# Giving out the side work of the last two-path block in finer pieces, and reordering a second product

## The chip, the cores and the metric

The kernel runs on one core of one Trainium2 chip. The metric is the device time of one execution in microseconds (us), from a launch that does everything on the chip: the inputs lie in device memory, and the output is written back to it. TensorE (PE) does the matrix products, VectorE (DVE), ScalarE (ACT) and GpSimd (POOL) the elementwise work, and SyncE (SP) issues most transfers. The engines run side by side, each through its own list of instructions in order, and wait for one another by semaphores.

## The reference, cut to what matters

```python
def reference(...):                       # B = 2, S = 768, D = 512, 8 heads of 64
    x = attention(q, k, v)                # local window of 96 and 8 global keys
    # layer 1
    u = x + (U V applied along the sequence, rank 32)
    x = u + relu(u @ w_ch1) @ w_ch2       # w_ch1 512 x 2048, w_ch2 2048 x 512
    # layer 2
    u = x + real(fft(fft(x, axis=1), axis=2))
    un = (u - mean) / sqrt(var + 1e-6)
    return u + relu(un @ w_ch1') @ w_ch2'
```

The tokens of both batches are 1536 rows, cut into 12 tiles of 128: tiles 0 to 5 are batch 0, tiles 6 to 11 batch 1.

## The kernel before

**Precision.** A product of two float32 operands is made from three products of rounded parts: high by high, high by low, low by high. So every operand is split: a rounded copy (the "hi" tile, on ACT) and the rest (the "lo" tile, on DVE or POOL by a subtraction). Names: `wh`, `wo` are the parts of a weight tile, `gh`, `gl` of the relu's output, `uT..` of the transposed tokens.

**Blocks and chunks.** `ffn` walks over chunks c = 0 to 63 of 16 chunks a block; a block is four token tiles (512 tokens). Chunks 0 to 47 are layer 1, blocks 0 to 2, and chunks 48 to 63 are layer 2, block 0 (tiles 0 to 3, all of batch 0). A chunk has 12 matmuls at L201, which fill one accumulator `ps_h`, then ACT makes `gh` (L208) and DVE `gl` (L209) from it; and 12 matmuls at L224, which add the chunk before to the four accumulators `ps_acc`. So chunk c's L201 runs ahead of chunk c-1's L224. `w_split` makes a chunk's weights ready: ACT `wh` (L171), then POOL `wo` (L174, two pieces). `ffn` is a generator that stops four times a chunk.

**The other eight tiles of layer 2** (4 to 11) are not run as blocks but as the "unit" at the end (`unit`): 512 tokens stand for tiles 4 to 7 and 512 for tiles 8 to 11, and a scheme of the Strassen kind makes the first product of both from seven products of half matrices. Those need, from each pair of tiles (4+i, 8+i), the sums T1 to T4 of halves of the transposed tokens, split in hi and lo in the tiles `op0`, `op1`. The unit takes eight rounds p of two weight chunks. A round has 42 matmuls of the first product (L948), then four relus, q = 0 to 3, and 48 matmuls of the second product (L994): for each of eight tiles t and each of two weight chunks f three matmuls, which read relu number `f * 2 + t // 4`. The four `ps_acc` buffers hold the sums, and DVE adds each to `xall` (L1000), or in the last round makes the output (L252, L256) and sends it.

**Work beside a block.** `drive` runs `ffn` for 64 steps, a block, and lets a second generator, the side work, advance by `per` pieces per step on the average. During layer 2, block 0 the side work is the transform of batch 1 (`fft(1)`: 23 pieces, after a few empty ones of `lead`, which waits until layer 1 is done), and then `unit_tokens`, which normalizes, transposes and splits tiles 4 to 11. The names of the transform: `fold` makes on DVE, from sums and differences of the rows (L743, L746, L725, L726, L730), the operands `ee` and `oo` (hi by ACT L733, lo by DVE L738); PE multiplies them with tables (L775, L779, L786, L799, later L812, L825). `norm_one` takes mean and variance on DVE (L849, L850), the root on POOL (L851, L852), and writes the normalized tile `vb` on DVE (L854) into one of two halves of the buffer `vb0`; PE transposes it (L273 in `transpose_in`, L888 for the second tile of a pair); ACT copies the halves to `qk` (L882, L889, L890); POOL makes T1 to T4 (L892 to L895); ACT and DVE split them (L899, L900).

**Order.** The order in which the program is written is not quite the order of the engines: a scheduler goes over it and places each instruction in its engine's list, taking ready work ahead of work whose inputs it expects later. Instructions marked `keep` stay in the order written. All matmuls of `unit` are so marked; those of `ffn` and of the side work are not.

Of the kernel before, what the change touches and what calls it, by code (L numbers as in the profile page):

```python
# [10 lines left out]
ALU = mybir.AluOpType  # L11
AF = mybir.ActivationFunctionType

P = 128
B, H, S, HD = 2, 8, 768, 64
D = H * HD
# [4 lines left out]
NF = FF // P  # L21
# [17 lines left out]
class Prog:  # L39
# [801 lines left out]
        nc.vector.tensor_tensor(X[0:1, 511:256:-1], pc[0:1, 1:256], xm[0:1, 511:256:-1], ALU.add)  # L841
        yield

    def norm_one(self, i):
        nc, cp = self.nc, self.cp
        X = self.x[i]
        bs = cp.tile([P, 6], F32, tag="bs", bufs=2, name=f"bs{i}")
        mv = cp.tile([P, 2], F32, tag="mv", bufs=2, name=f"mv{i}")
        nc.vector.bn_stats(bs, X)  # L849
        nc.vector.bn_aggr(mv, bs)  # L850
        nc.gpsimd.tensor_scalar(mv[:, 1:2], mv[:, 1:2], 1.0e-6, None, ALU.add)  # L851
        nc.gpsimd.tensor_tensor(mv[:, 1:2], mv[:, 1:2], self.mh, ALU.pow)  # L852
        un = self.vb[0][:, (i % 2) * D:(i % 2 + 1) * D]
        nc.vector.tensor_scalar(un, X, mv[:, 0:1], mv[:, 1:2], ALU.subtract, ALU.mult)  # L854
        return un

    def norm(self, tiles):
        for i in tiles:
            un = self.norm_one(i)
            yield  # L860
            self.transpose_in(1, i, un)
            yield
# [5 lines left out]
    def unit_open(self, ctx):  # L868
        self.op = ctx.enter_context(self.tc.tile_pool(name="op", bufs=1))
        self.opu = [self.op.tile([P, 10, 512], FR, name=f"op{z}") for z in range(2)]  # L870

    def unit_tokens(self):
        nc = self.nc
        for i in range(4):
            st = self.qkb[i % 2]
            q0, q1 = st[:, 0:256], st[:, 256:512]
            T1, T2, T3, T4, b22 = (st[:, 512 + z * 256:768 + z * 256] for z in range(5))
            b12 = st[:, 1792:2048]
            un = self.norm_one(4 + i)
            yield  # L880
            tp = self.transpose_in(1, 4 + i, un)
            nc.scalar.copy(st[:, 0:512], tp)  # L882
            yield
            un = self.norm_one(8 + i)
            yield
            tp = self.psum("tr")
            for dd in range(ND):
                nc.tensor.transpose(tp[:, dd * P:(dd + 1) * P], un[:, dd * P:(dd + 1) * P], self.ident)  # L888
            nc.scalar.copy(b12, tp[:, 0:256])  # L889
            nc.scalar.copy(b22, tp[:, 256:512])  # L890
            yield
            nc.gpsimd.tensor_tensor(T1, b12, q0, ALU.subtract)  # L892
            nc.gpsimd.tensor_tensor(T3, b22, b12, ALU.subtract)
            nc.gpsimd.tensor_tensor(T2, T3, q0, ALU.add)
            nc.gpsimd.tensor_tensor(T4, q1, T2, ALU.subtract)  # L895
            yield
            hi, lo = (t[:, :, i * P:(i + 1) * P] for t in self.opu)
            src = st[:, 512:1792].rearrange("p (n q) -> p n q", n=10)
            nc.scalar.copy(hi, src)  # L899
            nc.vector.tensor_tensor(lo, src, hi.bitcast(F32), ALU.subtract)  # L900
            yield

    def unit_load(self, p):
# [28 lines left out]
    def unit(self):  # L932
        nc, keep = self.nc, self.tc.keep_in_program_order
# [7 lines left out]
        for p in range(NF // 2):  # L941
# [20 lines left out]
            X, Z, Y = self.psum("h"), self.psum("h"), self.psum("m")  # L962
# [20 lines left out]
            self.unit_load(p + 2)  # L983
            wh, wo = self.uw[p, 2]
            acc = {}
            order = [(0, 1), (1, 1), (0, 0), (1, 0)] + [(t, f) for t in range(2, 8) for f in (0, 1)]
            for t, f in order:
                first = t not in acc
                if first:
# [13 lines left out]
def drive(main, n, side, per):  # L1003
    acc = 0.0
    for _ in range(n):
        next(main)
        acc += per
        while acc >= 1.0 and side is not None:
            acc -= 1.0
            if next(side, "end") == "end":  # L1010
                side = None
    if side is not None:
        drain(side)


def lead(pg, n):
    while pg.n_done < n:
        yield


def chain(*gens):
    for g in gens:
        if callable(g):
            g = g()
        if g is not None:
            yield from g


def arm(tc, pg, fast):
# [59 lines left out]
    with ExitStack() as ctx4, ExitStack() as ctx3:  # L1089
        pg.fft_open(ctx3)  # L1090
        drive(main, 64, chain(pg.tr_gen(0, range(8, 12), pg.x), pg.fft_tables()), 0.3)
        drive(main, 64, chain(lead(pg, 6), pg.fft(0), pg.norm(range(0, 4))), 0.58)
        drive(main, 64, chain(lead(pg, 12), pg.fft(1), lambda: (ctx3.close(), pg.unit_open(ctx4), None)[2],
                              pg.unit_tokens()), 0.85)
        drain(main)


# [5 lines left out]
def drain(g):  # L1103
    for _ in g:
        pass


def program(tc, a):
    with ExitStack() as ctx:
        pg = Prog(tc, a)  # L1110
        pg.open(ctx)

        pg.setup(ctx)
        rv = tc.nc.values_load(pg.flag[0:1, 0:1], min_val=0, max_val=1)
        with tc.If(rv > 0) as cmp:
            arm(tc, pg, True)
        with cmp.Else():
            arm(tc, pg, False)
# [114 lines left out]
```

## Time and profile before

| | before |
|---|---|
| median of 3 runs | 685.51 us (681.99 to 686.04) |
| profiled execution, its time | 685.0 us |
| its span, first to last instruction | 683.1 us |
| mean granted TensorE clock | 0.992 |
| PE busy | 653.2 us (96%) |
| DVE busy | 420.3 us (62%) |
| ACT busy | 298.2 us (44%) |
| POOL busy | 334.6 us (49%) |

The profile is of one execution; 1.9 us of its time lie outside the span. An engine's busy time is the union of its instructions' spans; matmuls overlap one another, since one starts before the one ahead has left the array, so the pitch from start to start says what a matmul costs. In this execution, layer 2, block 0 takes from about 396 us to 511 us, and the unit from 511 us to the end.

### The profile page before, as it was taken

The numbers are of one execution on the slowest core, as the hardware profiler recorded it, in microseconds if no ns is written. First come the engines' busy times: TensorE is split into PE (matmuls) and PEld (weight loads), VectorE is DVE, ScalarE is ACT, GpSimd is POOL, SyncE is SP. The second block draws the span as 40 slices with busy tenths as digits, with TensorE's granted clock in tenths as the row PEclk, the third lists the DMA queues.
The fourth block names the chain that finished last, engine by engine and source line by source line (L and its number), as shares of the span: only waits on it lengthen the run. The fifth ranks groups of instructions, "written<-read, shape, count | busy, mean of one in ns | idle before, by whom it ended". The sixth has DMA issues, their size and how long they took to land.

```text
span 683.1 us, 9548 instructions
## 1 busy us (share of the span) xinstructions
PE 653.2 (96%) x3442; PEld 535.2 (78%) x3442; DVE 420.3 (62%) x770; ACT 298.2 (44%) x586; POOL 334.6 (49%) x336
## 2 busy tenths in 40 slices
PE   5998899999999999999999999999889999999996
PEld 4877686888778888888887777887668888888885
DVE  4789778998839534396388574474434544554544
ACT  4879874544435434344334323234433442224420
POOL 4002403546676555555356564357676644656410
PEclk8999999999999999999999999999999999999999
DMA  5588715778896877666463652111002111011003
GB/s 201 202 322 303 244 48 156 238 249 253 284 343 201 259 258 253 233 220 214 162 211 128 251 191 87 62 62 61 32 35 90 62 62 48 15 62 61 1 2 128
DMA packets 32841, 107.50 MB, mean 157 GB/s; under 512 B 3920, under 2 KB 6160, under 8 KB 29712
## 3 DMA queue, kind: packets, MB, share of 16 engines
q1 hardware_dynamic: 31248, 103.01, 44.2%
q0 software_dynamic: 1392, 3.65, 1.7%
q8 instruction: 29, 0.48, 0.3%
q14 instruction: 28, 0.23, 0.1%
q10 hardware_dynamic: 144, 0.13, 0.1%
HBM read 86.75 MB, written 20.02 MB: 156 GB/s over the span
## 4 chain that ended last, share of the span: by engine, by line
PE 53%; DVE 10%; POOL 6%; issue 3%; ACT 2%; DMA 2%; SPq 0%; DVEq 0%; POOLq 0%; ACTq 0%
PE ps_acc L994 13%; PE ps_acc L224 13%; PE ps_h L201 13%; PE ps_h L948 10%; POOL wo L174 2%; DVE wr L160 2%; DVE w L162 2%; PE ps_sd L948 2%; DVE gl L209 1%; DMA ur<-wscr 1%; ACT wr L156 1%; PE ps_sd L799 1%; PE ps_sd L775 1%; DMA w<-wscr 1%; POOL mv L852 1%
## 5 line engine op out<-in xcount | busy, mean ns | idle before, releaser
L174 POOL TENSOR_TENSOR wo<-w,wh 128x512 fp32r<-128x512 f32 x128 | 188.5, 1495 | 151.6 <-ACT wh L171 144.7
L201 PE MATMUL ps_h<-uT,wh 128*128 128x512 f32 x512 | 160.2, 393 | 0.4 <-DVE xall L592 0.4
L171 ACT CAST wh<-w 128x1024 fp32r<-128x1024 f32 x64 | 67.4, 1053 | 115.7 <-PE ps_acc L224 50.4
L201 PEld LDWEIGHTS ps_h<-uT,wh 128*128 128x128 f32 x512 | 94.5, 188 | 20.1 <-issue 1.6
L224 PE MATMUL ps_acc<-wh,gl 128*128 128x512 f32 x256 | 101.3, 396 | 2.4 <-DVE gl L209 2.1
L201 PE MATMUL ps_h<-uT,wo 128*128 128x512 f32 x256 | 100.4, 392 | 3.0 <-POOL wo L174 3.0
L224 PE MATMUL ps_acc<-wh,gh 128*128 128x512 f32 x256 | 102.0, 398 | 1.2 <-ACT gh L208 1.2
L224 PE MATMUL ps_acc<-wo,gh 128*128 128x512 f32 x256 | 100.3, 392 | 0.0
L209 DVE SCALAR_TENSOR_TENSOR gl<-ps_h,gh 128x512 fp32r<-128x512 f32 x64 | 43.8, 685 | 78.1 <-ACT gh L208 77.9
L929 POOL TENSOR_TENSOR uo<-ur,uh 128x256 fp32r<-128x256 f32 (+1 forms) x40 | 41.8, 1053 | 65.2 <-ACT uh L926 65.2
L208 ACT ACTIVATE gh<-ps_h 128x512 fp32r<-128x512 f32 x64 | 38.2, 597 | 61.4 <-PE ps_h L201 61.4
L224 PEld LDWEIGHTS ps_acc<-wh,gl 128*128 128x128 f32 x256 | 48.3, 189 | 15.3 <-DVE gl L209 5.0
L201 PEld LDWEIGHTS ps_h<-uT,wo 128*128 128x128 f32 x256 | 48.0, 188 | 15.0 <-POOL wo L174 4.7
L1000 DVE TENSOR_TENSOR xall<-ps_acc,xall 128x512 f32<-128x512 f32 x56 | 38.7, 692 | 32.9 <-PE ps_acc L994 32.8
L224 PEld LDWEIGHTS ps_acc<-wh,gh 128*128 128x128 f32 x256 | 48.5, 189 | 10.8 <-ACT gh L208 1.6
L224 PEld LDWEIGHTS ps_acc<-wo,gh 128*128 128x128 f32 x256 | 48.6, 190 | 9.7 <-issue 0.2
L160 DVE SCALAR_TENSOR_TENSOR wr<-wr 128x1024 int32<-128x1024 int32 x32 | 47.4, 1482 | 10.6 <-ACT wr L156 9.5
L537 ACT ACTIVATE p<-p,m 128x256 f32<-128x256 f32 (+2 forms) x96 | 47.6, 498 | 8.9 <-DVE m L525 8.9
L926 ACT CAST uh<-ur 128x256 fp32r<-128x256 f32 (+1 forms) x40 | 18.8, 488 | 74.9 <-PE ps_acc L994 68.9
L948 PE MATMUL ps_h<-op,uh 128*128 128x512 f32 x160 | 49.8, 392 | 0.0
L525 DVE CUSTOM_DVE_ANT_0 p<-ps_acc,dist 128x256 f32<-128x256 f32 (+2 forms) x96 | 34.9, 419 | 3.2 <-ACT pt L555 1.9
L156 ACT ACTIVATE wr<-wr 128x1024 f32<-128x1024 f32 x32 | 36.7, 1147 | 0.0
(263 smaller groups left out, 1142.4 us busy)
## 6 DMA issues: line engine op xcount, KB each, us to landing
w<-wscr SPq DMA_DIRECT2D x48, 512.0 KB, 4.3
wr<-wl SPq DMA_DIRECT2D x17, 1024.0 KB, 8.2
wr<-wl SPq DMA_DIRECT2D x60, 256.0 KB, 5.4
wscr<-w SPq DMA_DIRECT2D x16, 512.0 KB, 9.0
wscr<-wd SPq DMA_DIRECT2D x16, 512.0 KB, 3.0
ur<-wscr SPq DMA_DIRECT2D x16, 512.0 KB, 4.4
qk<-qkg SPq DMA_DIRECT2D x7, 1088.0 KB, 7.4
vb<-vw SPq DMA_DIRECT2D x8, 768.0 KB, 5.0
```

The lines of the kernel that those rows point to most:

```text
L156: keep(nc.scalar.activation(hi.bitcast(F32), hi.bitcast(F32), AF.Copy, scale=2.0 ** -112))
L160: nc.vector.scalar_tensor_tensor(lo, hi, 3, lo, ALU.logical_shift_left, ALU.bitwise_or)
L171: nc.scalar.copy(hi, raw)
L174: nc.gpsimd.tensor_tensor(lo[:, h], raw[:, h], hi[:, h].bitcast(F32), ALU.subtract)
L201: nc.tensor.matmul(hp, lhsT=w[:, s], rhs=u[:, dd, :], start=n == 0, stop=n == 11)
L209: nc.vector.scalar_tensor_tensor(gl, hp, 0.0, gh.bitcast(F32), ALU.max, ALU.subtract)
L224: nc.tensor.matmul(acc[t], lhsT=g[:, s], rhs=w[:, D:2 * D], start=pf == 0 and m == 0, stop=pf == NF - 1 and m == 2)
L537: keep(nc.scalar.activation(T[z][:, s], T[z][:, s], AF.Exp, bias=m[:, z, y:y + 1], scale=-1.0, accum_out=sm[:, u % 2, y, z:z + 1]))
L929: nc.gpsimd.tensor_tensor(lo[:, s], src, hi[:, s].bitcast(F32), ALU.subtract)
L948: keep(nc.tensor.matmul(out, lhsT=x[:, s], rhs=y[:, kt, :], start=start and kt + n == 0, stop=kt + n == 3, skip_group_check=not start))
L994: keep(nc.tensor.matmul(acc[t], lhsT=x[:, s], rhs=y[:, w], start=first and n == 0, stop=not first and n == 2))
L1000: nc.vector.tensor_tensor(self.x[4 + t], acc[t], self.x[4 + t], ALU.add)
```

## The change

Four things change.

1. The rate of the side work beside layer 2, block 0 goes from 0.85 to 1.25 pieces a step. The transform, whose 23 pieces are as they were, so takes 18 steps in place of 27.
2. `unit_tokens` was five steps for each of four pairs of tiles, a pair after the other. It is now 24 steps over all eight tiles, each followed by an empty piece (48 pieces), in an order in which tile k+1 is normalized (N) ahead of tile k's transposition (X), and the sums (T) and the split (H) of a pair come later still.
3. T1 to T4 are made on DVE in place of POOL. And `norm_one` takes the half of `vb0` from its caller: the two tiles of a pair had the same half, now they have one each.
4. In the unit's second product the three-matmul groups go in runs of four tiles: tiles 0 to 3 with the second chunk (f = 1), the same with the first, then tiles 4 to 7 likewise. In the last round tiles 4 to 7 are still finished one by one.

```diff
-    def norm_one(self, i):
+    def norm_one(self, i, z):
...
-        un = self.vb[0][:, (i % 2) * D:(i % 2 + 1) * D]
+        un = self.vb[0][:, z * D:(z + 1) * D]
...
     def unit_tokens(self):
         nc = self.nc
-        for i in range(4):
+        un = {}
+
+        def parts(i):
             st = self.qkb[i % 2]
-            un = self.norm_one(4 + i)
-            yield
-            tp = self.transpose_in(1, 4 + i, un)
-            nc.scalar.copy(st[:, 0:512], tp)
-            yield
-            un = self.norm_one(8 + i)
-            yield
...
-            nc.gpsimd.tensor_tensor(T1, b12, q0, ALU.subtract)
-            nc.gpsimd.tensor_tensor(T3, b22, b12, ALU.subtract)
-            nc.gpsimd.tensor_tensor(T2, T3, q0, ALU.add)
-            nc.gpsimd.tensor_tensor(T4, q1, T2, ALU.subtract)
-            yield
+        def N(k):
+            un[k] = self.norm_one(4 + k // 2 + k % 2 * 4, k % 2)
+
+        def X(k):
...
+        def T(i):
+            st, (q0, q1, T1, T2, T3, T4, b22, b12) = parts(i)
+            nc.vector.tensor_tensor(T1, b12, q0, ALU.subtract)
+            nc.vector.tensor_tensor(T3, b22, b12, ALU.subtract)
+            nc.vector.tensor_tensor(T2, T3, q0, ALU.add)
+            nc.vector.tensor_tensor(T4, q1, T2, ALU.subtract)
+
+        def H(i):
...
+        for n in "N0 N1 X0 N2 X1 T0 N3 X2 H0 N4 X3 T1 N5 X4 H1 N6 X5 T2 N7 X6 H2 X7 T3 H3".split():
+            {"N": N, "X": X, "T": T, "H": H}[n[0]](int(n[1]))
+            yield
             yield
...
-            order = [(0, 1), (1, 1), (0, 0), (1, 0)] + [(t, f) for t in range(2, 8) for f in (0, 1)]
+            order = [(t, f) for f in (1, 0) for t in range(4)]
+            if p < NF // 2 - 1:
+                order += [(t, f) for f in (1, 0) for t in range(4, 8)]
+            else:
+                order += [(t, f) for t in range(4, 8) for f in (1, 0)]
...
-                              pg.unit_tokens()), 0.85)
+                              pg.unit_tokens()), 1.25)
```

Neither the number of PE's instructions nor their shapes change. How the lists of the engines differ is shown at three places; the number behind a name is that of the chunk, of the tile or of the batch, and the one after the underscore a running number of the buffer.

PE, where the first product of the transform of batch 1 (L775) stands, before: behind all of chunk 50's L201 and chunk 49's L224.

```order
L224 MATMUL ps_acc_3886<-wh49_3802,gh49_3874 128x512
L224 MATMUL ps_acc_3886<-wo49_3803,gh49_3874 128x512
L224 MATMUL ps_acc_3886<-wh49_3802,gl49_3875 128x512
L775 MATMUL ps_sd_3973<-c10_2160,ee1_3859 128x386
L775 MATMUL ps_sd_3973<-c11_2161,ee1_3859 128x386
L775 MATMUL ps_sd_3973<-c10_2160,ee1_3859 128x386 x2
L775 MATMUL ps_sd_3973<-c11_2161,ee1_3859 128x386
L201 MATMUL ps_h_3986<-uT100_3565,wh51_3905 128x512
```

The same in the changed kernel:

```order
L201 MATMUL ps_h_3933<-uT100_3565,wo50_3855 128x512
L775 MATMUL ps_sd_3951<-c10_2160,ee1_3845 128x386
L775 MATMUL ps_sd_3951<-c11_2161,ee1_3845 128x386
L775 MATMUL ps_sd_3951<-c10_2160,ee1_3845 128x386 x2
L775 MATMUL ps_sd_3951<-c11_2161,ee1_3845 128x386
L201 MATMUL ps_h_3933<-uT100_3565,wh50_3854 128x512
```

It now stands in the middle of chunk 50's L201, 18 matmuls of 512 columns earlier; DVE's and ACT's lists ahead of it are nearly as they were.

DVE, the last pairs of the tokens' part, before:

```order
L900 TENSOR_TENSOR op1_4289<-qk0_64,op0_4288 128x10x128
L854 TENSOR_SCALAR vb0_68<-xall1_186,mv11_4635 128x512
L276 TENSOR_TENSOR uT111_4304<-ps_sd_4610,uT110_4303 128x4x128
L209 SCALAR_TENSOR_TENSOR gl61_4625<-ps_h_4603,gh61_4624 128x512
L900 TENSOR_TENSOR op1_4289<-qk1_65,op0_4288 128x10x128
L209 SCALAR_TENSOR_TENSOR gl62_4677<-ps_h_4659,gh62_4676 128x512
L209 SCALAR_TENSOR_TENSOR gl63_4720<-ps_h_4706,gh63_4719 128x512
```

The same in the changed kernel, where the last tile's `vb` stands six rows ahead of the first row shown:

```order
L209 SCALAR_TENSOR_TENSOR gl60_4579<-ps_h_4561,gh60_4578 128x512
L276 TENSOR_TENSOR uT111_4253<-ps_sd_4601,uT110_4252 128x4x128
L209 SCALAR_TENSOR_TENSOR gl61_4630<-ps_h_4616,gh61_4629 128x512
L898 TENSOR_TENSOR qk1_65<-qk1_65 128x256
L899 TENSOR_TENSOR qk1_65<-qk1_65 128x256
L900 TENSOR_TENSOR qk1_65<-qk1_65 128x256
L901 TENSOR_TENSOR qk1_65<-qk1_65 128x256
L908 TENSOR_TENSOR op1_4211<-qk1_65,op0_4210 128x10x128
L209 SCALAR_TENSOR_TENSOR gl62_4677<-ps_h_4659,gh62_4676 128x512
L209 SCALAR_TENSOR_TENSOR gl63_4720<-ps_h_4706,gh63_4719 128x512
```

The split (L900 before, L908 now) no longer stands right ahead of a `vb` (L854), and the four sums (L898 to L901) have come to DVE.

POOL, the same place, before:

```order
L174 TENSOR_TENSOR wo62_4597<-w62_4539,wh62_4596 128x512 x2
L174 TENSOR_TENSOR wo63_4655<-w63_4601,wh63_4654 128x512 x2
L892 TENSOR_TENSOR qk1_65<-qk1_65 128x256
L893 TENSOR_TENSOR qk1_65<-qk1_65 128x256
L894 TENSOR_TENSOR qk1_65<-qk1_65 128x256
L895 TENSOR_TENSOR qk1_65<-qk1_65 128x256
L929 TENSOR_TENSOR uo00_4699<-ur0_4541,uh00_4698 128x256
```

And in the changed kernel:

```order
L174 TENSOR_TENSOR wo60_4499<-w60_4450,wh60_4498 128x512 x2
L174 TENSOR_TENSOR wo61_4549<-w61_4503,wh61_4548 128x512 x2
L174 TENSOR_TENSOR wo62_4610<-w62_4553,wh62_4609 128x512 x2
L174 TENSOR_TENSOR wo63_4655<-w63_4614,wh63_4654 128x512 x2
L941 TENSOR_TENSOR uo00_4699<-ur0_4555,uh00_4698 128x256
```

POOL's sums for the last pair, which stood behind the low part of chunk 63's weights, are gone from its list.

## Rows read from the trace of the kernel before

**Rows 1.** PE's waits, 395 to 512 us: us in total, times, longest.

```profile
PE ps_sd L888 <- DVE vb L854: 2.2, 2, 1.2
PE ps_sd L775 <- ACT ee L733: 1.7, 1, 1.7
PE ps_acc L224 <- ACT gh L208: 1.2, 1, 1.2
PE ps_h L201 <- POOL wo L174: 1.0, 1, 1.0
PE ps_acc L224 <- DVE gl L209: 0.9, 1, 0.9
```

**Rows 2.** Stretches: us, busy of PE, PEld, DVE, ACT, POOL, PEclk, DMA share, GB/s.

```profile
398.00:413.00 15.00, 14.04 (x64) 11.46 (x62) 14.94 (x26) 4.98 (x9) 8.85 (x10) 1.00 0.54 193
450.00:500.00 50.00, 46.82 (x220) 37.69 (x219) 26.30 (x39) 20.04 (x32) 35.45 (x43) 1.00 0.14 52
500.00:512.00 12.00, 9.88 (x36) 7.36 (x35) 5.52 (x7) 5.19 (x11) 7.80 (x10) 0.86 0.11 40
512.00:600.00 88.00, 88.00 (x383) 71.38 (x382) 41.95 (x60) 31.66 (x65) 49.29 (x52) 1.00 0.16 60
```

**Rows 3.** Timeline of PE at the transform's start: start us, us, what.

```profile
404.00 0.61 PE L201 MATMUL ps_h<-uT,wh 128*128 128x512 f32 x2
...
409.44 1.04 PE L775 MATMUL ps_sd<-c,ee 128*128 128x386 f32 x5
...
413.75 0.91 PE L775 MATMUL ps_sd<-c,ee 128*128 128x386 f32 x3 [1.71 <-ACT ee L733]
```

**Rows 4.** Timeline of DVE, the same stretch.

```profile
405.73 1.51 DVE L725 TENSOR_TENSOR qk<-qk 128x255 f32<-128x255 f32 x1
407.16 1.25 DVE L726 COPY qk<-qk 128x2 f32<-128x2 f32 x1
...
412.15 0.68 DVE L209 SCALAR_TENSOR_TENSOR gl<-ps_h,gh 128x512 fp32r<-128x512 f32 x1
412.75 0.41 DVE L725 TENSOR_TENSOR qk<-qk 128x255 f32<-128x255 f32 x1
```

**Rows 5.** Timelines of POOL and of ACT, the same stretch.

```profile
405.38 3.00 POOL L174 TENSOR_TENSOR wo<-w,wh 128x512 fp32r<-128x512 f32 x2 [0.21 <-ACT wh L171]
...
408.44 0.41 ACT L733 CAST ee<-qk 128x258 fp32r<-128x258 f32 x1 [3.14 <-DVE qk L726]
```

**Rows 6.** Timeline of PE, the tokens' part: its waits, and a slow stretch behind them.

```profile
468.82 0.66 PE L888 MATMUL ps_sd<-ident,vb 128*128 128x128 f32 x4 [0.97 <-DVE vb L854]
...
479.66 0.50 PE L201 MATMUL ps_h<-uT,wo 128*128 128x512 f32 x1 [0.96 <-POOL wo L174]
...
492.57 0.66 PE L888 MATMUL ps_sd<-ident,vb 128*128 128x128 f32 x4 [1.25 <-DVE vb L854]
...
502.65 0.50 PE L224 MATMUL ps_acc<-wh,gh 128*128 128x512 f32 x1 [1.22 <-ACT gh L208]
...
504.28 0.50 PE L224 MATMUL ps_acc<-wh,gl 128*128 128x512 f32 x1 [0.90 <-DVE gl L209]
...
505.53 0.63 PE L224 MATMUL ps_acc<-wh,gh 128*128 128x512 f32 x1
505.96 0.63 PE L224 MATMUL ps_acc<-wo,gh 128*128 128x512 f32 x1
```

**Rows 7.** Timelines of ACT and DVE, the last pair of the tokens' part.

```profile
500.84 1.26 ACT L899 CAST op<-qk 128x1280 fp32r<-128x1280 f32 x1 [5.12 <-POOL qk L895]
502.01 0.59 ACT L208 ACTIVATE gh<-ps_h 128x512 fp32r<-128x512 f32 x1
...
502.13 1.49 DVE L900 TENSOR_TENSOR op<-qk,op 128x1280 fp32r<-128x1280 f32 x1 [7.17 <-ACT op L899]
```

**Rows 8.** POOL's sums by line: duration ns min/median/max, first and last start.

```profile
L895 POOL TENSOR_TENSOR qk<-qk x4: 731/736/742, 463.1 to 500.1; 128x256 f32<-128x256 f32 x4
```

**Rows 9.** The page, part 5: us busy, mean ns, idle before.

```profile
L1000 DVE TENSOR_TENSOR xall<-ps_acc,xall 128x512 f32<-128x512 f32 x56 | 38.7, 692 | 32.9 <-PE ps_acc L994 32.8
```

More of the change, by code (lines that the diff above doesn't have):

```diff
@@ L858, in norm @@
         for i in tiles:
-            un = self.norm_one(i)
+            un = self.norm_one(i, i % 2)
             yield
@@ L873, in unit_tokens @@
         nc = self.nc
-        for i in range(4):
+        un = {}
+        def parts(i):
             st = self.qkb[i % 2]
-            q0, q1 = st[:, 0:256], st[:, 256:512]
-            T1, T2, T3, T4, b22 = (st[:, 512 + z * 256:768 + z * 256] for z in range(5))
-            b12 = st[:, 1792:2048]
-            un = self.norm_one(4 + i)
-            yield
-            tp = self.transpose_in(1, 4 + i, un)
-            nc.scalar.copy(st[:, 0:512], tp)
-            yield
-            un = self.norm_one(8 + i)
-            yield
-            tp = self.psum("tr")
+            return st, [st[:, z * 256:z * 256 + 256] for z in range(8)]
+        def N(k):
+            un[k] = self.norm_one(4 + k // 2 + k % 2 * 4, k % 2)
+        def X(k):
+            st, (q0, q1, T1, T2, T3, T4, b22, b12) = parts(k // 2)
+            if k % 2 == 0:
+                tp = self.transpose_in(1, 4 + k // 2, un.pop(k))
+                nc.scalar.copy(st[:, 0:512], tp)
+                return
+            u, tp = un.pop(k), self.psum("tr")
             for dd in range(ND):
-                nc.tensor.transpose(tp[:, dd * P:(dd + 1) * P], un[:, dd * P:(dd + 1) * P], self.ident)
+                nc.tensor.transpose(tp[:, dd * P:(dd + 1) * P], u[:, dd * P:(dd + 1) * P], self.ident)
             nc.scalar.copy(b12, tp[:, 0:256])
             nc.scalar.copy(b22, tp[:, 256:512])
-            yield
-            nc.gpsimd.tensor_tensor(T1, b12, q0, ALU.subtract)
-            nc.gpsimd.tensor_tensor(T3, b22, b12, ALU.subtract)
-            nc.gpsimd.tensor_tensor(T2, T3, q0, ALU.add)
-            nc.gpsimd.tensor_tensor(T4, q1, T2, ALU.subtract)
-            yield
+        def T(i):
[5 more added lines that the diff above has]
+        def H(i):
+            st, _ = parts(i)
             hi, lo = (t[:, :, i * P:(i + 1) * P] for t in self.opu)
```

## Prediction

> **What bounds the kernel now.** I looked first at the busy time by stretch, then at PE's waits in the block that the change touches, then at the timelines around each wait. In the unit PE is busy for all of the 88 us from 512 to 600 us at the full granted clock [rows 2], so no wait there has anything to give. In layer 2, block 0 it is not: PE loses 3.2 of 50 us in the tokens' part and 2.1 of 12 us at its end, where the granted clock is 0.86 as well [rows 2]. PE's number of matmuls is the same in both kernels, so the change is worth what it does to waits, and to the clock behind them. The view of waits lists all that PE waits for between 395 and 512 us: 2.2 us for normalized tiles (`vb`), 1.7 for the transform's operand `ee`, 1.2 for `gh`, 1.0 for `wo`, 0.9 for `gl`, together 7.0 [rows 1].
>
> **What the change removes: the tokens' part.** Both waits for `vb` (0.97 and 1.25 us [rows 6]) come about since `vb` (L854) stands in DVE's list behind the split (L900), which waits for ACT's cast (L899), and that for POOL's sums: at the last pair ACT waits 5.12 us for POOL, and DVE 7.17 us for ACT [rows 7]. In the new order a tile's `vb` comes a whole step earlier, and its half of the buffer is not the one that the tile ahead still holds. Following the new lists by hand, with 0.227 us for a matmul of 512 columns (24 of them between 404.00 and 409.44 us [rows 3]), every `vb` but the first is done more than 5 us ahead of its transposition. So 2.2 us go. The wait for `wo` (0.96 us [rows 6]) came of POOL's list: four sums of 0.74 us [rows 8], 2.9 us, stood between the weight splits. They are gone from it, so 1.0 us goes.
>
> At the end of the block the chain is T on POOL, cast on ACT until 502.10, `gh` on ACT behind it (502.01), `gl` on DVE behind the split that starts at 502.13 [rows 7]; PE waits 1.22 us for the one and 0.90 for the other. Then the clock falls: two neighbouring matmuls start 0.43 us apart (505.53 and 505.96 [rows 6]) where the usual pitch is 0.227. The stretch's clock of 0.86 over 12 us [rows 2] is 3.4 us at 1.2 in place of 2.4 GHz, 1.7 us of work. In the new kernel T stands on DVE right behind ACT's copies, where nothing else queues. In the trace ACT had made the copies of the last pair 3.15 us after its transposition (492.57 [rows 6]) began, at 500.84 - 5.12 = 495.72 [rows 7]. The four sums take 4 x 0.41 = 1.6 us, by the fold's sum of nearly the same shape on DVE [rows 4], or up to 6 us if each meets a POOL instruction as the same line does at 405.73 (1.51 us [rows 4]). I take the short ones, since POOL's own sums are gone and its weight splits so end sooner. Cast 1.26 and `gh` 0.59 follow [rows 7]: `gh` of chunk 62 is there 6.6 us after the transposition, and PE wants it after four transposes (0.4 us) and 36 matmuls (8.2 us), 2.0 us later. `gl` needs split 1.49 [rows 7] and 0.68 [rows 4] after the cast, 8.2 us, and is wanted 0.45 us after `gh`, 0.8 us later. So both waits go, the second with little to spare, and with them the reason for the clock to fall: 1.2 + 0.9 + 1.7 = 3.8 us. I leave 0.4 us for new waits over the whole part (bounds 0 and 2: none by the lists, or both waits at the end as they were). Removed in all: 2.2 + 1.0 + 3.8 = 7.0 us, less 0.4.
>
> **What it costs: the transform's start.** At 1.25 pieces a step the first L775 stands 18 matmuls, 4.1 us, earlier in PE's list: behind six L201 that start at 404.00, so at 405.36 in place of 409.44 [rows 3]. Its operands come no earlier, since DVE is busy for 14.94 of the 15 us from 398 to 413 us [rows 2] and its list is the same up to there. The fourth matmul wants the second third of `ee`, which ACT has at 408.44 + 0.41 = 408.85 [rows 5]. PE is there at 405.36 + 3 x 0.18 = 405.9 (five of them took 1.04 us [rows 3]): a wait of 3.0 us where there was none. Then come two L775, six L201 (1.4 us), one more L775 at about 410.7 (0.2 us of wait for its low part), four L224 (0.9 us), and the L775 on the last third of `ee`. That was ready at 413.75 [rows 3]; in the new list the fold's sum L725 takes the place of `gl` at 412.15 in place of 412.75 [rows 4], so 0.6 us earlier, 413.15. PE is there at 411.85: a wait of 1.3 us in place of 1.71. Together 3.0 + 0.2 + 1.3 = 4.5 us against 1.7, so 2.8 us more. The later products (L812, L825) also come closer together, with two `ps_sd` buffers that ACT and DVE must empty between them; by the lists two of these come out even, at 0 to 0.6 us each, and I take 0.3 us.
>
> The clock is the open term here. In this trace single waits of 1.71, 1.25 and 0.97 us left it at the full rate, and two waits of 2.1 us together within some 3 us did not [rows 2, 6]. A single wait of 3.0 us is nearer to the latter, so I take a fall to 1.2 GHz of the same 3.4 us. Since PE waits 1.3 us in it anyway, it costs (3.4 - 1.3) / 2 = 1.1 us. Its bounds are 0 (no fall) and 1.7 us (all of it work). Cost in all: 2.8 + 0.3 + 1.1 = 4.2 us, from 2.5 to 6.
>
> **The second product in runs of four.** All four sums are now open at once. The first closes after 15 matmuls, is added on DVE in 0.69 us [rows 9], and its buffer is wanted nine matmuls or 2.0 us later: enough, and DVE's add of 0.69 us keeps up with three matmuls (0.68) over four tiles. The relu of the other chunk is wanted later than before, that of tiles 4 to 7 as before or later. As PE had no wait there [rows 2], this gives 0. In the last round four outputs go out at 0.7 us spacing and the last four as before, so the end is the same: 0.
>
> **Sum.** Against the profiled execution's 685.0 us: 685.0 - 7.0 + 0.4 + 4.2 = 682.6 us. The median of the runs, 685.51, is 0.5 us above it; waits end a little sooner than I count, since a matmul behind a wait takes 0.50 in place of 0.39 us [rows 6] and more waits go than come. I leave these two against each other and say 682.5 us, 0.4% faster.
>
> **Rivals.** First, long sums. Beside a pair of POOL's L174 (3.00 us at 405.38 [rows 5]) DVE's sum of 0.41 us took 1.51, and a copy of two columns 1.25 [rows 4], as if each waited for a POOL instruction to end. In the last pair one L174 pair can so hold two of the four sums, by 1.1 us each. That is 2.2 us against 0.8 of spare time for `gl` and 2.0 for `gh`: waits of 1.4 and 0.2 us come back, with them perhaps the clock's 1.7, and the time is 682.5 + 3.3 = 685.8 us. It decides from one held sum. For it speak rows 4; against it, that POOL's split for chunk 63 may be over by then. The Trainium skill has a rule for it (GPSIMD Engine Reference, "1. Specifications"): GpSimd's ways into SBUF are shared with VectorE, and DVE instructions with two SBUF inputs contend with it. It speaks against moving T to DVE, the trace agrees (1.51 against 0.41 us), and by it the time is this rival's, wherever the two meet.
>
> Second, DVE becomes the bound of the whole transform, and the kernel is slower than before. The hold of some 2.2 us per L174 pair, with the pairs of chunks 51 to 54 in 18 steps, falls on folds or on buffers that PE waits to have emptied. Two such hits more than I count give 682.5 + 4.4 = 686.9 us; from 3 us of them on the gain is gone. For it: DVE had no time left in the fold [rows 2]; against it: PE did not wait at the later products at all [rows 1].
>
> Third, the transform's start costs less: the clock doesn't fall (-1.1), and the scheduler's fillers hide the small waits (-0.5), with no new wait in the tokens' part (-0.4): 680.5 us; if the fold's held instructions [rows 4] also escape POOL, by 2.2 us, 678.3 us.
>
> Fourth, the change does not do what it says: the 1.7 us at the half clock and the waits in front of it hang on where the execution happens to stand, and the run of 681.99 us may be one without them. Then the median holds less to win: 684.5 us.
>
> **How the numbers follow.** Chances: forecast 0.47, long sums 0.10, DVE as the bound 0.10, cheaper start 0.23, little to win 0.10. A change of 1%, 6.9 us, is about what a measurement of this kernel can tell from none: faster than 678.7 is only the far end of the third case and a little of the forecast's own spread, 0.17; slower than 692.4 needs the first two rivals together and more, 0.04; within 1% is the rest, 0.79. The range takes in the cheap start down to 678.3 and the slow rivals up to 686.9.
>
> **What would show it.** Right: no wait of PE for `vb`, `wo`, `gh` or `gl` in the last 50 us of the block and a full clock at its end; a wait for `ee` of about 3 us at the first L775, a second of 1.3, and a stretch at half clock behind them; PE busy throughout the unit. Wrong: DVE's sums L898 to L901 at 1.5 us each in the last pair, waits at L812 or L825, or waits at the second product.

## The result and the profile after

The changed kernel takes 678.4 us in the median of seven runs (677.5 to 680.2), the kernel before 684.7 in seven runs beside it (682.0 to 686.0): a ratio of 0.992, with a 95% interval of 0.990 to 0.994. The slowest run of the changed kernel is faster than the fastest of the kernel before. The forecast was 682.5 us, so the direction was right and the time is 4.1 us below it, just inside the stated range, which begins at 678.3. The gain is 6.3 us; the forecast had 3.0, counted from the median of 685.51 that it knew. The profiled execution has a span of 676.3 us, against 683.1 before.

To compare stretches I cut each trace at two instructions that all kernels have: the first L201 of chunk 50 (404.00 us before, 403.34 after) and the first matmul of the unit (511.00 and 504.39). In between, called the block below, the changed kernel needs 101.05 us in place of 107.00. The rest moved little: 0.66 us ahead of the block, where the programs do the same work (in all the traces the block starts between 402.55 and 405.13 us), and 0.2 us in the unit (172.1 and 171.9 us to the end of the span).

PE's waits between 395 and 512 us of the changed kernel, which answer to [rows 1]; five entries have become one:

```profile
engine line waited for: us in total, times, longest us
PE ps_sd L775 <- ACT ee L733: 2.5, 1, 2.5
```

The busy time of each engine by stretch, which answers to [rows 2] (the seventh figure is PE's granted clock as a share):

```profile
398.00:413.00 15.00, 12.47 (x50) 9.70 (x49) 14.94 (x31) 5.81 (x11) 9.08 (x11) 0.89 0.49 177
450.00:500.00 50.00, 50.00 (x233) 41.34 (x232) 29.82 (x41) 24.43 (x38) 28.35 (x25) 1.00 0.18 64
500.00:512.00 12.00, 12.00 (x55) 9.85 (x54) 4.43 (x7) 5.59 (x12) 10.11 (x13) 1.00 0.37 136
```

The tokens' part and the block's end have lost all their waits and the slow clock. The start of the transform has become worse: PE is busy for 12.47 of 15 us where it had 14.04, and the clock there is 0.89. PE's timeline of that stretch answers to [rows 3]:

```profile
403.34 0.62 PE L201 MATMUL ps_h<-uT,wh 128*128 128x512 f32 x2
...
404.69 0.69 PE L775 MATMUL ps_sd<-c,ee 128*128 128x386 f32 x3
407.91 0.62 PE L775 MATMUL ps_sd<-c,ee 128*128 128x386 f32 x2 [2.53 <-ACT ee L733]
...
410.07 0.52 PE L775 MATMUL ps_sd<-c,ee 128*128 128x386 f32 x1
410.39 0.63 PE L224 MATMUL ps_acc<-wh,gh 128*128 128x512 f32 x1
410.81 0.63 PE L224 MATMUL ps_acc<-wo,gh 128*128 128x512 f32 x1
411.24 0.63 PE L224 MATMUL ps_acc<-wh,gl 128*128 128x512 f32 x1
411.67 0.63 PE L224 MATMUL ps_acc<-wh,gh 128*128 128x512 f32 x1
412.24 0.87 PE L775 MATMUL ps_sd<-c,ee 128*128 128x386 f32 x2
412.94 0.39 PE L224 MATMUL ps_acc<-wo,gh 128*128 128x512 f32 x1
```

There is one wait, of 2.53 us, at the first product; then matmuls start 0.43 us apart, 1.2 GHz, until about 412.8; and the second forecast wait, at the L775 on the last third of `ee` (412.24), is missing. ACT's cast of that third shows why; it answers to [rows 5], and is over at 412.19, just when PE, at the slow clock, comes to the product that needs it:

```profile
411.78 0.41 ACT L733 CAST ee<-qk 128x258 fp32r<-128x258 f32 x1 [0.81 <-DVE qk L727]
```

The timeline of PE, DVE, ACT and POOL at the block's end, which answers to [rows 7] (L892 is the last tile's transposition, L894 the last copy of it, and the sums are now DVE's L898 to L901):

```profile
490.33 0.60 PE L892 MATMUL ps_sd<-ident,vb 128*128 128x128 f32 x4
...
491.69 2.72 POOL L174 TENSOR_TENSOR wo<-w,wh 128x512 fp32r<-128x512 f32 x2 [2.51 <-ACT wh L171]
491.78 0.38 ACT L894 COPY qk<-ps_sd 128x256 f32<-128x256 f32 x1
491.92 1.35 DVE L898 TENSOR_TENSOR qk<-qk 128x256 f32<-128x256 f32 x1 [2.23 <-ACT qk L893]
493.19 1.51 DVE L899 TENSOR_TENSOR qk<-qk 128x256 f32<-128x256 f32 x1
494.73 0.43 DVE L900 TENSOR_TENSOR qk<-qk 128x256 f32<-128x256 f32 x1
495.19 0.43 DVE L901 TENSOR_TENSOR qk<-qk 128x256 f32<-128x256 f32 x1
495.71 1.26 ACT L907 CAST op<-qk 128x1280 fp32r<-128x1280 f32 x1 [3.55 <-DVE qk L901]
...
497.00 1.49 DVE L908 TENSOR_TENSOR op<-qk,op 128x1280 fp32r<-128x1280 f32 x1 [1.38 <-ACT op L907]
...
498.41 0.69 DVE L209 SCALAR_TENSOR_TENSOR gl<-ps_h,gh 128x512 fp32r<-128x512 f32 x1
...
499.40 0.39 PE L224 MATMUL ps_acc<-wh,gl 128*128 128x512 f32 x1
```

The first two sums ran beside a pair of POOL's weight splits (L174) and took three times as long as the others. So the four sums took 3.7 us and not the 1.6 of the forecast. But ACT's copies were done 1.83 us after the transposition began (490.33 to 492.16), where the forecast had 3.15. PE took up `gl` at 499.40, 0.3 us after it was there. The first rival's mechanism was present, and fell just short of a wait.

### The profile page after: what moved, and what is told of

It reads as the page before. It is cut to its first block, busy times and chain, and to the rows that moved or that the text cites. A ratio compares the mean times of both kernels' runs of the same rounds, so it can differ in the third digit from the quotient of the medians.

```text
span 676.3 us, 9536 instructions
## 1 busy us (share of the span) xinstructions
PE 651.8 (96%) x3442; PEld 536.2 (79%) x3442; DVE 425.9 (63%) x786; ACT 299.5 (44%) x586; POOL 323.9 (48%) x320
## 4 chain that ended last, share of the span: by engine, by line
PE 62%; DVE 7%; DMA 2%; POOL 2%; ACT 2%; issue 1%; SPq 0%; DVEq 0%; ACTq 0%; POOLq 0%
PE ps_acc L224 17%; PE ps_h L201 17%; PE ps_acc L1010 13%; PE ps_h L960 10%; DVE wr L160 2%; DVE w L162 2%; PE ps_sd L960 2%; ACT wr L156 1%; PE ps_sd L775 1%; PE ps_sd L799 1%; DMA ur<-wscr 1%; DMA wscr<-wd 1%; POOL wo L174 1%; DMA w<-wscr 1%; PE ps_sd L273 1%
## 5 line engine op out<-in xcount | busy, mean ns | idle before, releaser
L174 POOL TENSOR_TENSOR wo<-w,wh 128x512 fp32r<-128x512 f32 x128 | 188.6, 1495 | 158.9 <-ACT wh L171 143.8
L201 PE MATMUL ps_h<-uT,wh 128*128 128x512 f32 x512 | 160.4, 394 | 0.4 <-DVE xall L592 0.4
L201 PEld LDWEIGHTS ps_h<-uT,wh 128*128 128x128 f32 x512 | 94.4, 188 | 19.9 <-issue 1.6
L201 PE MATMUL ps_h<-uT,wo 128*128 128x512 f32 x256 | 100.4, 392 | 2.1 <-POOL wo L174 2.1
L224 PE MATMUL ps_acc<-wh,gl 128*128 128x512 f32 x256 | 100.7, 393 | 1.4 <-DVE gl L209 1.1
L224 PE MATMUL ps_acc<-wh,gh 128*128 128x512 f32 x256 | 101.5, 396 | 0.0
L224 PE MATMUL ps_acc<-wo,gh 128*128 128x512 f32 x256 | 100.0, 391 | 0.0
L209 DVE SCALAR_TENSOR_TENSOR gl<-ps_h,gh 128x512 fp32r<-128x512 f32 x64 | 43.8, 684 | 75.6 <-ACT gh L208 75.5
L224 PEld LDWEIGHTS ps_acc<-wh,gl 128*128 128x128 f32 x256 | 48.2, 188 | 13.7 <-DVE gl L209 3.6
L201 PEld LDWEIGHTS ps_h<-uT,wo 128*128 128x128 f32 x256 | 48.1, 188 | 13.3 <-POOL wo L174 3.0
L224 PEld LDWEIGHTS ps_acc<-wh,gh 128*128 128x128 f32 x256 | 48.4, 189 | 9.4 <-issue 0.2
L224 PEld LDWEIGHTS ps_acc<-wo,gh 128*128 128x128 f32 x256 | 48.3, 189 | 9.4 <-issue 0.2
```

What stands on the lines that cost most here:

```text
L174: nc.gpsimd.tensor_tensor(lo[:, h], raw[:, h], hi[:, h].bitcast(F32), ALU.subtract)
L201: nc.tensor.matmul(hp, lhsT=w[:, s], rhs=u[:, dd, :], start=n == 0, stop=n == 11)
L209: nc.vector.scalar_tensor_tensor(gl, hp, 0.0, gh.bitcast(F32), ALU.max, ALU.subtract)
L224: nc.tensor.matmul(acc[t], lhsT=g[:, s], rhs=w[:, D:2 * D], start=pf == 0 and m == 0, stop=pf == NF - 1 and m == 2)
```

## Experiments

Each time is the median of 5 to 12 runs. The change has four parts: the pace, the order of the tokens' part (with one half of `vb0` for each tile of a pair, which no run takes apart from the order), the place of the sums, and the unit's order. (The old tokens' part gives out six pieces a pair, 24 in all, as many as the new one without its empty pieces; the five steps named above are one too few.) The experiments take the parts apart, and then turn to the start of the transform. Theory: the tokens' part gains by its order and by the sums' place, and the pace costs time at the transform. Rivals: one of these parts is the whole of it; the pace is needed.

**e1, new tokens' part at the old pace**

```diff
             {"N": N, "X": X, "T": T, "H": H}[n[0]](int(n[1]))
             yield
-            yield
...
-                              pg.unit_tokens()), 1.25)
+                              pg.unit_tokens()), 0.85)
```

> The changed kernel with the transform handed out at the old pace (0.85 pieces per step, one piece of the tokens' part per yield instead of a piece and an empty one). The order of the tokens' part, its sums on DVE and the unit's order are the new ones. Theory A (the gain is the new order of the tokens' part, the cost is the denser transform): PE waits for the transform's inputs about 1.7 us once, as before, the clock stays at 2.4 GHz there, no wait comes back in the tokens' part, and the time is 678.4 - 2.5 = 675.9 us (675.3 to 676.8). Rival B (the tokens' part needs the wider spacing of 1.6 steps per piece; at 1.18 the waits come back): 678 to 681, with waits for vb, gh or gl in the tokens' part.

Measured: 677.5 us (675.6 to 679.2), ratio 0.9885 (0.985 to 0.992). PE's only wait is the old one of 1.71 us for `ee`, the clock is 1.00 throughout, and the block takes 98.69 us, 2.36 less than with the change. In the medians 0.9 us of this is seen, and the intervals overlap. Theory A holds for the block: the pace costs 2.4 us there and buys nothing. That the whole kernel gains 2.4 us without it, the times do not show.

**e2, old tokens' part at the new pace**: the kernel before, with a second `yield` behind each of the six in `unit_tokens`, and 1.25 for 0.85.

> The kernel before, with only the new pace: 1.25 pieces per step, and an empty piece behind each piece of the old tokens' part, so that transform and tokens' part stand as densely as in the changed kernel; old order, sums on POOL, old order of the unit. Theory A: the transform's start costs its 2.5 us more (wait for ee some 2.5 us, then a stretch at 1.2 GHz), the waits for vb (1.0 to 1.25 us each) shrink by the 0.6 us that each piece gains, and the tail keeps part of its waits: 685 to 687 us, slower than before. Rival B (the spacing alone takes the waits away): 678 to 681 us.

Measured: 683.8 us (682.8 to 687.1), ratio 0.999 (0.997 to 1.001). The wait of 2.53 us and the slow stretch are there, the waits for `vb` are gone, 2.6 us of waits for `gh`, `gl` and `wo` remain, and a second slow stretch stands at 472.4 us, in place of that at 505. The spacing takes about as much away as it costs; it is not the gain.

**e3, a gap ahead of the first product**: the changed kernel, with three empty pieces between folds and products.

```diff
         c1, s1, c2, s2 = ([ct[n + "0"], ct[n + "1"]] for n in ("c1", "s1", "c2", "s2"))
+        for _ in range(3 * b):
+            yield
```

> The changed kernel with three empty pieces between the folds of the second transform and its first product, nothing else. Theory A (the 2.5 us are a wait of the first product for the folds, and the clock falls because of that wait): both waits of PE in the block go, no stretch at 1.2 GHz follows, and the time is 678.4 - 2.5 - up to 2.2 (what is left of the wait and the clock) = 674.5 to 676.3 us. Rival C (the clock falls there by itself with the denser transform, or the time comes back as other waits later, since the tokens' part ends 2.4 steps later): 677.5 to 678.5 us.

Measured: 678.7 us (678.4 to 680.1), ratio 0.990 (0.988 to 0.993), the block 100.99 us: no gain, as rival C had it. Its lines are read below, with e8.

**e4, sums back on POOL**: the changed kernel, `nc.gpsimd` for `nc.vector` in the four lines of T.

> The changed kernel with the four sums of each pair of tiles back on POOL, all else new. Four sums took 4 x 0.736 = 2.9 us there, and a piece of the tokens' part is given out every 2.5 us. Theory A (the order carries the tokens' part, the move of the sums the end of the block): the waits for vb stay away, but at the block's end H3 waits for POOL again, and 1 to 2.1 us of waits for gh and gl with 1.7 us of slow clock come back: 680 to 682 us. Rival D (the wider spacing would have been enough with the sums on POOL): 678 to 679 us.

Measured: 682.9 us (681.6 to 686.4), ratio 0.997 (0.995 to 0.999); 4.5 us of the change's 6.3 are gone. PE's waits in the block:

```profile
PE ps_sd L775 <- ACT ee L733: 3.6, 2, 2.5
PE ps_acc L224 <- DVE gl L209: 2.4, 3, 0.9
PE ps_acc L224 <- ACT gh L208: 0.2, 1, 0.2
```

Not one pair but three wait, the last as it did before: ACT's cast waits 5.13 us for POOL's last sum, `gh` stands behind it, and DVE's split, with `gl` behind it, waits for the cast. The timeline at the last pair:

```profile
500.32 1.26 ACT L907 CAST op<-qk 128x1280 fp32r<-128x1280 f32 x1 [5.13 <-POOL qk L901]
501.49 0.59 ACT L208 ACTIVATE gh<-ps_h 128x512 fp32r<-128x512 f32 x1
501.62 1.49 DVE L908 TENSOR_TENSOR op<-qk,op 128x1280 fp32r<-128x1280 f32 x1 [8.23 <-ACT op L907]
```

**e5, the sums alone**: the kernel before, `nc.vector` for `nc.gpsimd` in the four lines of T.

> The kernel before with only the four sums of each pair moved from POOL to DVE; old pace, old order of the tokens' part, old order of the unit. Theory A (the sums cost the waits for gh, gl and wo with the slow clock at the end, 4.8 us by the prediction's terms; the order costs the waits for vb, 2.2 us, which stay): 684.5 - 4.8 = 679.7 us (679 to 681), with waits for vb left. Rival D (the sums are the whole of it, and the new order does nothing, so that the old pace keeps the transform cheap): 676 to 677.5 us, as the changed kernel with the old pace (677.5).

Measured: 677.5 us (675.5 to 678.9), ratio 0.989 (0.986 to 0.992). Theory A falls, and rival D holds: one word in four lines of the kernel before does all that the change does. The waits for `vb` went too, though the order is the old one. They came, as the prediction's chain had it, through the split that waits for POOL's sums; with the sums short, that chain is cut at its root. The block takes 100.30 us, with a slow stretch behind the wait of 1.71 us that had none in the kernel before (read below).

**e6, old pace and a gap**: e1 with two empty pieces at e3's place.

> The changed kernel at the old pace (0.85, no empty pieces in the tokens' part), with two empty pieces between the folds of the second transform and its first product. At the old pace the first product waited 1.7 us once, for the third fold; two pieces are 2.4 steps, 18 matmuls or 4.1 us of PE work put ahead of it. Theory A (DVE's chain of folds sets that wait; more PE work ahead of the product takes it away, and nothing later takes its place): no wait of PE in the block, clock 1.00 throughout, 677.5 - 1.7 = 675.8 us, and the block some 97.0 us from its start to the unit instead of 98.7. Rival C (as with the gap at the new pace, the time comes back as a slow clock or a later wait): 677 to 678 us, the block 98 us or more.

Measured: 675.1 us (673.7 to 676.0), ratio 0.985 (0.983 to 0.988): the fastest of all, and the interval lies apart from that of the change. No wait of PE in the block, the clock 1.00, the block 97.02 us, as theory A said.

**e7, old order in the unit**: the changed kernel with the old list of (t, f).

> The changed kernel with the old order of the unit's second product (pairs of two tiles), all else new. Theory A (the order of the unit's products is worth nothing, since no matmul there waits): 678.4 us within 0.7, the unit 171.9 us within 0.3. Rival F (runs of four spare PE something at each change of half): 1 us or more slower, the unit 173 us.

Measured: 679.5 us (678.8 to 680.7) beside a before of 685.2, ratio 0.992 (0.990 to 0.995), that of the change. The unit takes 172.2 us, the block 100.86. The 0.3 us by which the units differ are less than what the unit differs by among kernels that all have the new order (171.8 us in e1, 172.5 in e11), so no worth of the runs of four is seen.

**e8, copies of the folds on ACT**: the changed kernel, one line of `fold`.

```diff
-                nc.vector.tensor_copy(f[0:rows, 0:257:256], E[:, 0:257:256])
+                (nc.scalar.copy if b else nc.vector.tensor_copy)(f[0:rows, 0:257:256], E[:, 0:257:256])
```

> The changed kernel with the two-column copies of the second transform's folds on ACT instead of DVE (on DVE they took 0.16, 1.22, 0.16 and 0.20 us in a stretch in which DVE never idled), nothing else. Theory G (the chain of folds on DVE sets when the third fold is there, and with it what the denser transform costs; the slow clock there only fills the time): the third fold comes some 1.4 us earlier, and the time falls by 1.0 to 1.5 us, to 676.9 to 677.4 us. Rival H (the cost at the start of the transform is the wait for the second fold and the slow clock that follows it, whatever DVE does): 678 to 679 us; or ACT, with its casts of 1.06 us ahead, makes the copies late: 678.4 to 680 us.

Measured: 680.4 us (679.5 to 681.0), ratio 0.993 (0.991 to 0.996), the block 102.18 us: no gain, rather 1 us lost. DVE was not relieved, since other instructions came to lie beside POOL's pair. The timeline of the three engines:

```profile
408.71 3.00 POOL L174 TENSOR_TENSOR wo<-w,wh 128x512 fp32r<-128x512 f32 x2
408.82 1.76 DVE L743 TENSOR_TENSOR qk<-xall 128x512 f32<-128x512 f32 x1
...
410.51 1.48 DVE L738 TENSOR_TENSOR oo<-vb,oo 128x256 fp32r<-128x256 f32 x1
...
413.63 0.41 ACT L733 CAST ee<-qk 128x258 fp32r<-128x258 f32 x1 [0.47 <-DVE qk L727]
```

L743 takes 0.68 us elsewhere (at 399.00 us of the change's trace), and L738 0.41. So theory G was not tested by the shorter chain that it needed; but together with e3 the trace bears on it. Counted from the block's start, the last third of `ee` is there after 8.85 us in the change (412.19 - 403.34), 8.90 in e3 and 8.91 in e8 (414.04 - 405.13). What PE can do by then in the change and e8 is 16 matmuls of 0.227 us and six L775 of 0.176, 4.7 us; 4.2 us are lost, by a wait of 2.53 and a slow clock in the change, by waits of 0.57 and 3.27 in e8. (In e8 the slow clock came behind the third, and its block is 1.1 us longer.) In e3 the gap gave PE eight more matmuls to do by then (1.8 us), but the clock fell behind the third and not ahead of it. PE's timeline in e3:

```profile
410.45 1.50 PE L777 MATMUL ps_sd<-c,ee 128*128 128x386 f32 x6
413.96 0.67 PE L777 MATMUL ps_sd<-c,ee 128*128 128x386 f32 x2 [2.00 <-ACT ee L733]
...
415.60 1.06 PE L201 MATMUL ps_h<-uT,wh 128*128 128x512 f32 x2
416.45 0.63 PE L201 MATMUL ps_h<-uT,wo 128*128 128x512 f32 x1
416.88 1.05 PE L201 MATMUL ps_h<-uT,wh 128*128 128x512 f32 x2
```

From 414.4 to 417.8 us PE ran at 1.2 GHz, and half of these 3.4 us is what the gap had given. The trace of e4 bears this reading out. Up to there e4 is the changed kernel, with the same wait of 2.53 us, but its clock stayed at the full rate, and the second wait of the forecast is there:

```profile
412.98 0.63 PE L775 MATMUL ps_sd<-c,ee 128*128 128x386 f32 x2 [1.07 <-ACT ee L733]
```

This product starts 8.91 us after e4's block (404.07), and 8.90 after the change's. From the block's start to the matmul behind L787 e4 takes 14.61 us and the change 14.85: the slow clock cost 0.24 us there, since it ran in time that PE would have spent waiting. A kernel with a shorter chain of folds was not tried.

**e9, the sums and the gap**: e5 with e6's two empty pieces.

> The kernel before with the four sums of each pair on DVE, and two empty pieces between the folds of the second transform and its first product; old pace, old order of the tokens' part, old order of the unit. Theory A2 (where the sums run is the whole gain in the tokens' part; new order, new pace and the unit's order add nothing; the wait for the third fold is 1.7 us and a slow clock behind it in some runs): the time of the changed kernel at the old pace with the same gap, 0.985 of before, about 675 us (674 to 676), no wait of PE in the block. Rival J (the new order does give something, hidden so far by the slow clock in one kernel and not in the other): 1 us or more slower than that, 676 to 678 us, with waits for vb, gh or gl.

Measured: 677.8 us (677.1 to 678.7), ratio 0.990 (0.988 to 0.992), the block 98.58 us. Rival J holds: against e6, which differs by the two new orders (of which the unit's showed no worth in e7) and the halves of `vb0`, the block is 1.6 us longer. The gap moved the old tokens' part by 2.4 steps, and two waits of 0.5 us came up in it. The waits, in the block:

```profile
PE ps_sd L890 <- DVE vb L856: 0.5, 1, 0.5
PE ps_acc L224 <- DVE gl L209: 0.5, 1, 0.5
```

The `vb` stands behind a split of the pair ahead, and beside a pair of POOL's, as the timeline shows:

```profile
467.44 1.49 DVE L902 TENSOR_TENSOR op<-qk,op 128x1280 fp32r<-128x1280 f32 x1 [1.37 <-ACT op L901]
...
468.44 3.06 POOL L174 TENSOR_TENSOR wo<-w,wh 128x512 fp32r<-128x512 f32 x2 [3.17 <-ACT wh L171]
...
468.85 1.51 DVE L856 TENSOR_SCALAR vb<-xall,mv 128x512 f32<-128x512 f32 x1
```

**e10, the gap alone**: the kernel before with two empty pieces.

> The kernel before with two empty pieces between the folds of the second transform and its first product, nothing else: sums on POOL, old order, old pace. Theory A2: the wait of 1.7 us for the third fold goes, and the waits for vb, wo, gh and gl stay or change little: 684.8 - 1.7 = 683 us (682 to 684). Rival K (the gap is what made e6 fast: shifted by two pieces, the tokens' part meets POOL's splits elsewhere): 680 us or less.

Measured: 681.2 us (678.5 to 683.3), ratio 0.995 (0.993 to 0.997), the block 101.93 us in the profile. More than theory A2 gave, less than rival K. In the profile, of an execution of 679.3 us and so one of the faster of the eleven, the tail's waits and its slow clock were gone as well, while waits for `vb`, `gh` and `gl` of 4.0 us in all stood near 470 and 481 us. Moving the tokens' part by two pieces, without touching it, changes which pair is late.

**e11, the sums twice**: the changed kernel, T's four lines in `for _ in range(2)`.

> The changed kernel with the four sums of each pair computed twice over on DVE (the same results written again), nothing else. In the changed kernel gl of the last pair was there some 0.3 us before PE wanted it. The second round of sums takes 1.6 us (0.41 each) up to 3.7 us (beside POOL's splits, as in the last pair). Theory L (that margin is all there is; the sums' length on DVE decides at the end of the block): a wait for gl or gh of 1.3 us or more comes back at the end, perhaps with a slow clock: 680 to 682.5 us. Rival M (the margin is read wrongly, or the scheduler fills in): 678 to 679 us without a wait there.

Measured: 679.4 us (677.9 to 680.5), ratio 0.992 (0.990 to 0.995), the block 100.99 us, no wait at the end: rival M. The margin was not used up, because the scheduler reordered the lists: `gl` of chunk 62 (496.03) now stands ahead of the pair's cast (497.13) and split (498.43), not behind them. The timeline:

```profile
496.03 0.68 DVE L209 SCALAR_TENSOR_TENSOR gl<-ps_h,gh 128x512 fp32r<-128x512 f32 x1
...
497.13 1.27 ACT L908 CAST op<-qk 128x1280 fp32r<-128x1280 f32 x1 [3.28 <-DVE qk L902]
...
498.43 1.49 DVE L909 TENSOR_TENSOR op<-qk,op 128x1280 fp32r<-128x1280 f32 x1 [1.39 <-ACT op L908]
```

The 0.3 us is a margin of that list, not of the work.

**e12, the order alone**: e1 with the sums on POOL.

> The changed kernel at the old pace (0.85, no empty pieces) and with the sums back on POOL: of the tokens' part only the new order is left, beside the unit's new order, which made no difference. It closes the square at the old pace: old order and POOL 684.5 us, old order and DVE 677.5, new order and DVE 677.5. Theory A2 (the sums' place is nearly the whole gain; the new order alone takes the waits for vb away, 2.2 us, and leaves the casts that wait for POOL's sums and hold gh and gl behind them): 681 to 683.5 us, waits for gh or gl of 1 us or more each left. Rival N (either part alone removes the waits): 677 to 679 us.

Measured: 683.3 us (681.9 to 685.9), ratio 0.999 (0.998 to 1.001), the block 106.61 us. The waits for `vb` are gone, but the others, 6.0 us with that for `ee`, are not, and no gain is seen:

```profile
PE ps_acc L224 <- DVE gl L209: 1.8, 2, 0.9
PE ps_sd L775 <- ACT ee L733: 1.7, 1, 1.7
PE ps_acc L224 <- ACT gh L208: 1.2, 2, 1.0
PE ps_h L201 <- POOL wo L174: 1.0, 1, 1.0
PE ps_h L201 <- ACT wh L171: 0.3, 1, 0.3
```

At the old pace this closes the square:

| old pace | sums on POOL | sums on DVE |
|---|---|---|
| old order | 1 (before) | 0.989 (e5) |
| new order | 0.999 (e12) | 0.9885 (e1) |
| old order, gap | 0.995 (e10) | 0.990 (e9) |
| new order, gap | | 0.985 (e6) |

## Why the prediction was right, and where it was off

The forecast was added up from two large terms, -6.6 us for the tokens' part and +4.2 for the transform's start. Both had the right sign and, in the main, the right cause, and both were off to the same side, by 1.8 and 1.7 us.

**The tokens' part: mechanism right, 1.8 us too small, and credited to too many parts.** All four kinds of wait went, as said. The same stretch (from the matmul behind L787 to the unit) became 8.44 us shorter (87.82 to 86.20, less the 30 matmuls, 6.82 us, that now fall into it), where 7.0 - 0.4 = 6.6 were forecast. The waits are 5.3 us of it, and the slow clock at the end is 1.7, as counted. What is left, 1.4 us, was not counted. Most of it lies in how a wait is read: the view counts it from the end of the matmul ahead, 0.39 us after its start, though the next could have started after 0.227. So the two matmuls about the wait of 0.97 us (467.46 and 468.82) start 1.36 us apart, and the wait cost 0.16 more than it says. Behind three of the five waits the second matmul also came 0.335 us after the first, and not 0.227. The 0.4 us set aside for new waits did not come. That both `vb` waits and the end hang on POOL's sums stood in the prediction, but it took the order to be what removes the first. e5 shows that the place of the sums is enough for all of them, and e12 that the order without it takes the waits for `vb` away but gives no gain that is seen. What the order (with the halves of `vb0`) does give is 1.6 us where the tokens' part stands elsewhere (e9 against e6).

**The transform's start: right in kind, 4.2 forecast, 2.5 measured** (e1 confirms it by 2.36). The two waits of 3.0 and 1.3 us were priced, with 0.2 between them, at 2.8 us more than before, and the clock's fall at 1.1 on top. The runs show that DVE's folds set the end of this stretch: at the new pace the last third of `ee` is there about 8.9 us after the block's start, whatever PE does till then (9.7 at the old pace, whose list has a `gl` ahead of it). A slow clock ahead of that moment costs next to nothing, since PE would have waited (0.24 us, the change against e4); behind it, it costs its whole price (e3, e5). So the term of 1.1 us was the one too many: it was added to the second wait, but took that wait's place. The waits themselves are 2.53 and 1.07 us where the clock does not fall (e4); the first is shorter than the 3.0 forecast, as the second third of `ee` was there 4.52 us after the block's start and not 4.85. And the 0.3 us for the later products' buffers did not show: PE waited at none of them.

**The unit: 0 forecast, 0 measured** (e7).

**The first rival** (long sums beside POOL's splits) was there in the profile, at 3.7 us for the last four sums where it asked for 3.8, and so, for two of the four, was the prediction's own sign of being wrong. PE was not late all the same: of the 0.8 us of spare time forecast for `gl` 0.3 were left. The forecast was lucky here: the sums were 2.1 us longer than it said, but ACT's copies ahead of them came 1.3 us sooner than the 3.15 us that it took from the old trace, and without that `gl` would have been about 1 us late. The Trainium skill's rule behind it (GPSIMD Engine Reference, "1. Specifications": GpSimd shares its ways into SBUF with VectorE, and DVE instructions with two SBUF inputs contend) agrees with the trace (1.35 and 1.51 us beside POOL's pair, 0.43 behind it). It speaks against this move, and the move was still the whole gain, because on POOL the sums wait in line for those same splits. **The second rival** decided nothing: DVE did bound the first product, but not the later ones. **The third** came nearest, 680.5 to 678.3 us, and of its reasons some held: no new waits in the tokens' part, and hardly a price for the clock, though the clock did fall. Its last step, from 680.5 to 678.3, did not: the held instructions of the fold did not escape POOL (1.21 us for L725 and 1.22 for L726 beside a pair of splits, from 405.06 us). That the time came out there all the same is luck; the rest came from the time around the waits. **The fourth**, that there is little to win, is out: no run of the kernel before was as fast as any of the changed one.

**Sum.** -8.44 + 2.49 = -5.95 us in the block, as measured; -0.66 ahead of it and -0.2 in the unit are not of the change's making by anything seen here.

## What to carry to other kernels

Where a short job stands in an engine's list behind long ones, and a chain over two more engines hangs on it, moving that job to another engine can be worth more than reordering all the work around it; try that one line alone before the rest. Work that is given out at a denser pace comes up earlier in its engine's list, but its inputs are made no earlier: ask when the last input is there, and put other work ahead of the first use until then (e6). And when side work only shifts, its collisions shift too (e10, e9), so judge a reordering at more than one place.

## What the runs showed of the hardware

The clock's fall did not follow from the length of a wait alone. Behind the same wait of 2.53 us at the same two matmuls, the pitch went to 0.43 us in the changed kernel, e2, e7 and e11, but stayed at 0.23 in e4; behind the wait of 1.71 us it stayed in the kernel before and in e1, and fell in e5 and e12. PE in e5:

```profile
413.39 0.91 PE L775 MATMUL ps_sd<-c,ee 128*128 128x386 f32 x3 [1.71 <-ACT ee L733]
...
415.05 0.63 PE L201 MATMUL ps_h<-uT,wo 128*128 128x512 f32 x1
415.47 1.06 PE L201 MATMUL ps_h<-uT,wh 128*128 128x512 f32 x2
```

The slow stretch cost e5 some 1.6 us (seven matmuls at 0.427 us from start to start in place of 0.227, and two in between), and by so much its block is longer than e1's in the profiles; the medians agree. Executions of one kernel differ as well: of the 67 runs of the kernel before beside the experiments, the 23 with a mean granted clock of 0.994 took 683.2 us in the median, the 11 with 0.987 took 687.0. So one trace of each kernel can't tell whether a fall of the clock belongs to the kernel or to that execution. What decides was not found, and stays open; a price for the clock behind a wait is best given as a range from nothing to the whole.

DVE beside POOL's weight splits: not only sums of two inputs (0.41 to 1.51 us) and the 512-column fold (0.68 to 1.76) grew, but also the normalization of one tensor input (0.55 to 1.51, L854) and a copy of two columns (0.16 to 1.22, L726). They did not grow at every meeting, and `gl` (L209), which reads one of its two inputs from the accumulator, never did between 395 and 505 us of the changed kernel: 0.66 to 0.69 us, beside a pair or not.
